# A convolution and two feed-forward layers in split float32: all low parts on the vector engine, and couples of 64-row products from unit 50 on

## The chip, the cores and the metric

The kernel runs on one core of a Trainium2 chip. The metric is the device time of one execution in microseconds, taken as the median of three runs. The engines that matter here are TensorE (PE, with its weight loads as PEld), the vector engine (DVE), the scalar engine (ACT), GpSimd (POOL) and the DMA queue of the sync engine (SP). Each engine works through its own instructions in the order in which they stand in the program, and waits on semaphores for what other engines must have done.

## The reference

```python
def reference(x, weight, moe_w_in, moe_w_out, moe2_w_in, moe2_w_out):
    # x: 2 x 4096 tokens x 192 channels; weight: 8 heads x 7 taps
    w = softmax(weight, axis=-1)                        # per head
    x = causal_conv(x, w)                               # 7 taps over time, per channel
    h = x @ moe_w_in                                    # 192 -> 2048
    g = where(h >= 1, h, where(h <= -1, 0, (h + 1) ** 2 / 4))
    x = g @ moe_w_out                                   # 2048 -> 192
    h = x @ moe2_w_in                                   # 192 -> 2048
    g = h / (1 + exp(-1.702 * h))
    return g @ moe2_w_out                               # 2048 -> 192
```

The four weight matrices are float64 arrays when they reach the chip. They are brought to float32 there, bit by bit, and every float32 operand of a product is then split into a high part (the value rounded to the type that TensorE multiplies in one pass) and a low part (the value less its high part). A product of two operands is the sum of high by high, high by low and low by high.

## The kernel before, in words

**Tiles, units and phases.** The 8192 tokens are cut into 16 blocks of 512 tokens. Activations lie with channels on partitions: 128 channels (the a part) and the other 64 (the b part). The hidden width of 2048 is cut into 16 slices of 128. A *unit* is one slice of one block in one layer: `gemm1` makes the hidden tile `h` (128 x 512, in one of four PSUM banks, chosen by the unit's number), `act_a` applies the nonlinearity and writes the tile `a`, `act_b` splits it into `ghi` and `glo`, and `gemm2` adds its product to the two banks of the block's output. A *phase* is one block in one layer, so 16 units. `phases` begins with (layer 1, block 0), (1, 1), (1, 2), (2, 0). The first 64 units take two phases in turn, four units of the one and four of the other: units 0 to 31 are phases 0 and 1, units 32 to 63 are phases 2 and 3. From unit 64 on phases follow one after the other.

**Two ways to multiply.** A whole unit (`gemm1`, `gemm2`) has 5 products each, on all 128 rows of TensorE. The other way (`gemm1_pieces`, `gemm2_pieces`, woven together by `both`) cuts each product in two halves of 64 rows. Two halves, one on the lower and one on the upper 64 rows, run at the same time as a couple. As the b part has only 64 channels, 38 halves (19 couples) do the work that two units need 20 whole products for. For this a block's b part must stand in both orders, high part on the lower rows (tile `xb`) and high part on the upper rows (tile `xc`). `swap_halves` makes the second tile from the first by two DMAs on SP's queue, and only for phases at or after the bound in `put_b` and `finish`. In `both`, the lower list begins with the pieces of the first unit and then those of the second; the upper list begins with those of `gemm2`.

**The order of the work is written out by hand.** Step `u` of the first loop issues `gemm1(u)`, `act_a(u)`, `act_b(u-1)`, `gemm2(u-4)`, perhaps `finish` of a phase, and then what `plan` holds for this step (`beside`). So DVE's order in a step is: the last operation of the activation of `u` (L274 in layer 1, L277 in layer 2), the low part `glo` of `u-1` (where DVE makes it), the three operations of `finish`, and the planned work. From `WHOLE` on a second loop takes two units a turn: `both(u, u-4)`, then `act_a` of `u` and `u+1`, `act_b` of `u` and `u+1`, `finish`, and then `beside(u)` and `beside(u+1)`.

**Planned work.** `weight_ops` turns one slice of a layer's weights (a weight tile) from float64 into its two parts in four pieces, one in each of four steps in a row: `begin` (ACT L118, DVE L119 and L120), `join` (DVE L126), `high_part` (ACT L131) and `low_part` (L135 and L136, on the engine `eng`). The tiles 4 to 7 of layer 1 begin one a step in the steps 2 to 5; from tile 8 of layer 1 on one tile begins every second step, in step 2f-9 for tile f of layer 1 and in step 27+2f for tile f of layer 2, the last in step 57. So tile 11 of layer 2 has its `low_part` in step 52 and is first used by unit 55, and tile 15 has it in step 60 and is first used by unit 63. `conv_at(1)` puts 14 taps of the convolution (L156, L157) and two splits into the steps 10 to 25. `finish` of phase 0 (layer 1, block 0) is in the steps 32 to 34; its last split writes the `xb` that unit 36 reads. `finish` of phase 1 is in the steps 36 to 38.

**Who makes low parts.** `split` has ACT copy the high part and then DVE subtract it, or another engine if it is given one. In `act_b` that is POOL for the units below `EARLY` (48). For weight tiles it is DVE for tile 0 and the tiles 4 to 7 of layer 1 and the odd tiles of layer 2, and POOL for all others.

Of the kernel before, what the change touches and what calls it, by code (L numbers as in the profile page):

```python
# [20 lines left out]
def kernel(  # L21
# [21 lines left out]
    nc = tc.nc  # L43
    NBLK, D, _ = out.shape
    K = taps_in.shape[2]
    NF, _, WC = w1.shape
    DB = D - P
    B = P // DB
# [1 line left out]
    H = P // 2  # L50
    LAG = 4
    CH = 4
    WHOLE = 4 * NF
    EARLY = 3 * NF

    const = ctx.enter_context(tc.tile_pool(name="const", bufs=1))
    wpool = ctx.enter_context(tc.tile_pool(name="wpool", bufs=1))
# [12 lines left out]
    def f32(ap):  # L70
        return ap.bitcast(F32)

    def split(src, hi, lo, eng=None):
        nc.scalar.copy(hi, src)  # L74
        (eng or nc.vector).tensor_sub(lo, src, f32(hi))  # L75


    taps = const.tile([P, 2, K], F32, name="taps")
# [20 lines left out]
        nc.sync.dma_start(s.rearrange("p c t -> p (c t)"), words[n][f].bitcast(U32))  # L99
        return s  # L100

    def weight_ops(n, f, s, eng):

        low, high = s[:, :, 0], s[:, :, 1]  # L110
        w = wt[n][:, f, :]
        m = WC - DB
        st = {}

        def begin():
            a = stage.tile([P, WC], F32, tag="wa", name="wa")
            d = stage.tile([P, WC], U32, tag="wd", name="wd", bufs=3)
            nc.scalar.mul(a, f32(high), 2.0**-112)  # L118
            nc.vector.tensor_single_scalar(d, low, 29, op=ALU.logical_shift_right)  # L119
            nc.vector.scalar_tensor_tensor(  # L120
                d, high, 0x80000000, d, op0=ALU.bitwise_and, op1=ALU.bitwise_or
            )
            st["a"], st["d"] = a, d

        def join():
            nc.vector.scalar_tensor_tensor(  # L126
                st["d"], st["a"].bitcast(U32), 3, st["d"], op0=ALU.logical_shift_left, op1=ALU.bitwise_or
            )

        def high_part():  # L130
            nc.scalar.copy(w[:, 0:WC], f32(st["d"]))  # L131

        def low_part():
            d = f32(st["d"])
            eng.tensor_sub(w[:, WC + DB : 2 * WC], d[:, 0:m], f32(w[:, 0:m]))  # L135
            eng.tensor_sub(w[:, WC : WC + DB], d[:, m:WC], f32(w[:, m:WC]))  # L136

        return [begin, join, high_part, low_part]

# [3 lines left out]
    def new_xs():  # L143
        return [xs_p.tile([P, T], F32R, tag=t, name=t) for t in ("xah", "xal", "xb", "xc")]
# [16 lines left out]
    def warm_up():  # L161

        w = bank(7, "warm")
        for _ in range(9):
            nc.tensor.matmul(w[:, 0:P], ident, ident, start=True, stop=True)
# [15 lines left out]
    def swap_halves(dst, src):  # L181
        nc.sync.dma_start(f32(dst[0:DB]), f32(src[DB:P]))
        nc.sync.dma_start(f32(dst[DB:P]), f32(src[0:DB]))

    def put_b(i, c):

        b, halved = i % B, phases.index((1, i)) * NF >= WHOLE
        t = x1[i][2 + (b if halved else 0)]
        hi, lo = (t[0:DB], t[DB:P]) if b == 0 else (t[DB:P], t[0:DB])
        split(c[b * DB : (b + 1) * DB], hi, lo)  # L190
        if halved:
            swap_halves(x1[i][3 - b], t)
# [22 lines left out]
    phases = [(1, 0), (1, 1), (1, 2), (2, 0)]  # L215
# [64 lines left out]
    def act_b(u):  # L280
        a = act.pop(u)
        hi = g_p.tile([P, T], F32R, tag="ghi", name="ghi")
        lo = g_p.tile([P, T], F32R, tag="glo", name="glo")
        split(a, hi, lo, nc.gpsimd if u < EARLY else nc.vector)
        halves[u] = (hi, lo)

    def acc_banks(p):
# [79 lines left out]
    def finish(p, step):  # L367
        n, i = phases[p]
        acc_a, acc_b = accs.pop(p)
        if n == 1:  # L370
            ah, al, b, c = x2[i] = new_xs()
            s = cv_p.tile([P, T], F32, tag="cva", name="s")
            nc.scalar.copy(s[0:DB], acc_b[DB:P])
            split(acc_a, ah, al)
            at(step + 1, lambda: nc.vector.tensor_add(s[0:DB], acc_b[0:DB], s[0:DB]))

            def put():
                split(s[0:DB], b[0:DB], b[DB:P])
                if phases.index((2, i)) * NF >= WHOLE:
                    swap_halves(c, b)  # L380

            at(step + 2, put)
        else:
            o = o_p.tile([P, 2, T], F32, tag="o", name="o")
            nc.scalar.copy(o[0:DB, 1], acc_b[DB:P])
            nc.scalar.copy(o[:, 0], acc_a)
            nc.vector.tensor_add(o[0:DB, 1], acc_b[0:DB], o[0:DB, 1])
            nc.sync.dma_start(out[i, 0:P], o[:, 0])
            nc.sync.dma_start(out[i, P:D], o[0:DB, 1])


    plan, xt, raw = {}, {}, {}

    def at(step, op):
        plan.setdefault(max(step, 0), []).append(op)

    def fetch_w(n, f):
        raw[n, f] = weight_load(n, f)

    def weights_at(n, f, eng):  # L400
        ops = []

        def piece():
            if (n, f) in raw:
                ops.extend(weight_ops(n, f, raw.pop((n, f)), eng))
            ops.pop(0)()

        return [piece] * 4

    def fetch_x(*which):  # L410
        for part, i in which:
            xt[part, i] = x_load(part, i)
# [11 lines left out]
    with tc.manual_schedule():  # L424
        nc.sync.dma_start(taps, taps_in)
        fetch_x((0, 0), (1, 0))
        fetch_w(1, 0)
        fetch_w(1, 1)
        fetch_x((0, 1))
        fetch_w(1, 2)  # L430

        make_identity(nc, ident)
        warm_up()
        softmax_taps()

        nc.scalar.activation(const.tile([P, 1], F32, name="table"), ident[:, 0:1], AF.Sigmoid)
        for i in range(B):
            x1[i] = new_xs()
        ca = cv_p.tile([P, T], F32, tag="cva", name="cva")
        cb_ps, ca_ps = bank(3, "cb_ps"), bank(2, "ca_ps")  # L440
        a0 = conv_taps(0, xt[0, 0], ca)
        b_ops = conv_on_pe(1, xt[1, 0], cb_ps, ident, nc.scalar.mul)
        a1 = conv_on_pe(0, xt[0, 1], ca_ps, ident, nc.gpsimd.tensor_scalar_mul)
        for op in b_ops:
            op()

        ws = [weight_ops(1, f, raw.pop((1, f)), nc.gpsimd if f else nc.vector) for f in range(CH - 1)]
        order = a0[0:3] + ws[0][0:1] + a0[3:5] + ws[0][1:3] + a0[5:7] + ws[0][3:4] + ws[1][0:1]
        order += [lambda: put_a(0, ca)] + ws[1][1:2] + [lambda: put_b(0, cb_ps)] + ws[1][2:] + ws[2]
        for op in order:  # L450
            op()
        fetch_w(1, 3)
        for k, op in enumerate(weights_at(1, 3, nc.gpsimd)):
            at(k // 2, op)
        for k, op in enumerate(a1):
            at((k + 2) // 3, op)
        at(1, lambda: put_b(1, cb_ps))
        at(2, lambda: put_a(1, ca_ps))

        def convert_at(n, f, steps):  # L460
            eng = nc.vector if (n, f) < (1, 2 * CH) or n == 2 and f % 2 else nc.gpsimd
            at(steps[0] - 3, lambda: fetch_w(n, f))
            for step, op in zip(steps, weights_at(n, f, eng)):
                at(step, op)

        for f in range(CH, NF):
            s = f - 2 if f < 2 * CH else 2 * f - 2 * CH - 1
            convert_at(1, f, range(s, s + 4))
        for f in range(NF):
            s = 2 * NF - 5 + 2 * f  # L470
            convert_at(2, f, range(s, s + 4))
        for j in range(1, NBLK // B):
            conv_at(j)

        def beside(step):
            for op in plan.get(step, []):
                op()

        def finish_if_last(u, step):
            if 0 <= u < len(units) and units[u][1] == NF - 1:  # L480
                finish(units[u][0], step)


        for step in range(WHOLE):
            gemm1(step)
            act_a(step)
            if step >= 1:
                act_b(step - 1)
            if step >= LAG:
                gemm2(step - LAG)  # L490
            finish_if_last(step - LAG - 1, step)
            beside(step)


        act_b(WHOLE - 1)
        for u in range(WHOLE, len(units) + LAG + 4, 2):
            v = u - LAG
            if u == WHOLE:
                finish_if_last(v - 1, u)
                gemm1(u)  # L500
                gemm2(v)
                gemm1(u + 1)
                gemm2(v + 1)
            elif u < len(units):
                both(u, v)
            elif v < len(units):
                gemm2(v)
                gemm2(v + 1)
            if u < len(units):
                for op in (act_a, act_b):  # L510
                    op(u)
                    op(u + 1)
            finish_if_last(v + 1, u + 1)
            for step in (u, u + 1):
                beside(step)
# [55 lines left out]
```

## Time and profile before

| what | value |
|---|---|
| median of 3 runs | 1163.39 us (1161.4 to 1163.95) |
| the profiled execution's own time | 1161.93 us |
| its span, first to last instruction | 1160.2 us |
| busy: PE, DVE, ACT, POOL | 1140.1, 898.7, 836.2, 108.9 us |
| granted TensorE clock, mean | 0.996 |

The page of the profile gives busy time of every engine over the span, a strip of 40 slices of 29 us, and groups of instructions. Busy time of PE is the time in which some product was in flight, and products overlap, so it does not show how many could have been started. The counts of products in a stretch do.

### The profile page before, as it was taken

What the parts mean: (1) busy time and instruction counts of PE and PEld (TensorE: products, weight loads), DVE (VectorE), ACT (ScalarE), POOL (GpSimd) and SP (SyncE); (2) the same over time, 40 slices, a digit from 0 to 9 for tenths busy, and PEclk for the clock granted to TensorE, in tenths of its full rate; (3) what the DMA queues carried; (4) which work ended last, traced back from release to release, by engine and by line L of the source; (5) the groups of instructions that cost most, each with busy time, mean ns of one, the idle gap of its engine ahead of it and who ended that gap; (6) DMA issues with size and microseconds to landing.
All of it is one profiled execution on the core that took longest, in us unless ns stands there. A gap on an engine that the chain in (4) does not pass through costs nothing.

```text
span 1160.2 us, 22918 instructions
## 1 busy us (share of the span) xinstructions
PE 1140.1 (98%) x9180; PEld 929.5 (80%) x9180; DVE 898.7 (77%) x1354; ACT 836.2 (72%) x1467; POOL 108.9 (9%) x99
## 2 busy tenths in 40 slices
PE   8988999999999999999999999999999999999998
PEld 5766788888888888888888888888888888888886
DVE  7998999678686886869768796777868688686765
ACT  6778787676867768676776867768686775867764
POOL 5677730000000000000000000000000000000000
PEclk9999999999999999999999999999999999999999
DMA  4321321010001000010000100001000100000000
GB/s 149 129 80 54 99 64 33 2 41 20 15 20 42 1 20 15 19 42 8 27 10 11 42 11 24 10 10 42 19 15 19 42 1 19 15 19 15 10 15 14
DMA packets 16378, 36.15 MB, mean 31 GB/s; under 512 B 2448, under 2 KB 2448, under 8 KB 16272
## 3 DMA queue, kind: packets, MB, share of 16 engines
q1 hardware_dynamic: 16272, 34.69, 10.1%
q8 instruction: 72, 1.18, 0.4%
q14 instruction: 34, 0.28, 0.1%
HBM read 21.05 MB, written 6.29 MB: 24 GB/s over the span
## 4 chain that ended last, share of the span: by engine, by line
PE 91%; DVE 3%; POOL 2%; ACT 2%; issue 1%; DMA 0%; SPq 0%; POOLq 0%; DVEq 0%; ACTq 0%
PE acc L359 44%; PE h L359 39%; PE h L250 4%; POOL glo L75 1%; PE acc L310 1%; PE acc L311 1%; PE acc L313 1%; PE acc L312 1%; PE acc L314 1%; DVE wd L126 1%; DVE wd L119 1%; POOL wt L135 0%; DVE a L274 0%; DVE wt L135 0%; DMA raw<-in_w_dram 0%
## 5 line engine op out<-in xcount | busy, mean ns | idle before, releaser
L359 PE MATMUL acc<-ghi,wt 64*128 64x512 f32 x2676 | 810.4, 386 | 0.0
L359 PE MATMUL h<-xah,wt 64*128 64x512 f32 x1784 | 688.9, 386 | 0.0
L359 PE MATMUL acc<-glo,wt 64*128 64x512 f32 x1784 | 658.7, 387 | 0.0
L359 PEld LDWEIGHTS acc<-ghi,wt 64*128 64x128 f32 x2676 | 455.9, 184 | 51.5
L74 ACT CAST ghi<-a 128x512 fp32r<-128x512 f32 x512 | 313.9, 616 | 109.6 <-DVE a L277 73.5
L359 PEld LDWEIGHTS acc<-glo,wt 64*128 64x128 f32 x1784 | 328.2, 184 | 37.8 <-DVE glo L75 2.8
L359 PEld LDWEIGHTS h<-xah,wt 64*128 64x128 f32 x1784 | 328.3, 184 | 35.3 <-issue 0.4
L359 PE MATMUL h<-xal,wt 64*128 64x512 f32 x892 | 344.4, 386 | 0.0
L75 DVE TENSOR_TENSOR glo<-a,ghi 128x512 fp32r<-128x512 f32 x464 | 313.1, 687 | 20.0
L274 DVE SCALAR_TENSOR_TENSOR a<-h,a 128x512 f32<-128x512 f32 x256 | 176.5, 689 | 154.4 <-ACT a L273 154.2
L359 PE MATMUL h<-xb,wt 64*128 64x512 f32 x669 | 223.9, 388 | 0.0
L359 PE MATMUL h<-xc,wt 64*128 64x512 f32 x669 | 222.8, 386 | 0.0
L277 DVE TENSOR_TENSOR a<-h,a 128x512 f32<-128x512 f32 x256 | 169.9, 686 | 55.1 <-ACT a L276 54.2
L276 ACT ACTIVATE a<-h 128x512 f32<-128x512 f32 x256 | 146.5, 594 | 82.9 <-PE h L359 77.3
L272 ACT ACTIVATE a<-h 128x512 f32<-128x512 f32 x256 | 151.0, 590 | 52.3 <-PE h L359 48.8
L359 PEld LDWEIGHTS h<-xal,wt 64*128 64x128 f32 x892 | 164.1, 184 | 17.4
L273 ACT ACTIVATE a<-a 128x512 f32<-128x512 f32 x256 | 161.8, 632 | 8.2
L359 PEld LDWEIGHTS h<-xc,wt 64*128 64x128 f32 x669 | 123.1, 184 | 16.6
L359 PEld LDWEIGHTS h<-xb,wt 64*128 64x128 f32 x669 | 122.3, 184 | 9.5
L75 POOL TENSOR_TENSOR glo<-a,ghi 128x512 fp32r<-128x512 f32 x48 | 67.2, 1405 | 40.1 <-ACT ghi L74 37.6
L157 DVE SCALAR_TENSOR_TENSOR cva<-xt,taps,cva 128x512 f32<-128x512 f32 x90 | 69.6, 773 | 1.3
L250 PE MATMUL h<-xah,wt 128*128 128x512 f32 x132 | 54.9, 416 | 8.5 <-POOL wt L135 5.6
(70 smaller groups left out, 719.5 us busy)
## 6 DMA issues: line engine op xcount, KB each, us to landing
raw<-in_w_dram SPq DMA_DIRECT2D x32, 448.0 KB, 3.3
xc<-xb SPq DMA_DIRECT2D x42, 128.0 KB, 2.2
xt<-in_xa_dram SPq DMA_DIRECT2D x16, 259.0 KB, 3.2
out_dram<-o SPq DMA_DIRECT2D x16, 256.0 KB, 2.0
xt<-in_xb_dram SPq DMA_DIRECT2D x8, 259.0 KB, 3.1
out_dram<-o SPq DMA_DIRECT2D x16, 128.0 KB, 2.3
xb<-xc SPq DMA_DIRECT2D x14, 128.0 KB, 2.2
taps<-in_taps_dram SPq DMA_DIRECT2D x1, 7.0 KB, 1.6
```

Of the source, the lines that this page charges most:

```text
L74: nc.scalar.copy(hi, src)
L75: (eng or nc.vector).tensor_sub(lo, src, f32(hi))
L119: nc.vector.tensor_single_scalar(d, low, 29, op=ALU.logical_shift_right)
L126: nc.vector.scalar_tensor_tensor(st["d"], st["a"].bitcast(U32), 3, st["d"], op0=ALU.logical_shift_left, op1=ALU.bitwise_or)
L157: return lambda: nc.vector.scalar_tensor_tensor(c, x, w, c, op0=ALU.mult, op1=ALU.add)
L250: nc.tensor.matmul(h, w, r, start=j == 0, stop=j == len(prods) - 1)
L272: nc.scalar.activation(a, h, AF.Relu, bias=0.5, scale=0.5)
L273: nc.scalar.activation(a, a, AF.Square)
L274: nc.vector.scalar_tensor_tensor(a, h, 1.0, a, op0=ALU.max, op1=ALU.min)
L276: nc.scalar.activation(a, h, AF.Sigmoid, scale=1.702)
L277: nc.vector.tensor_mul(a, h, a)
L359: mm = nc.tensor.matmul(banks[n], w, r, start=n in fresh, stop=ends.get(n) == k)
```

## The change

The bound from which units run as couples, `WHOLE`, goes from 64 to 48, so that the second loop begins with unit 48 (its first turn is still of whole products, and `both` is first called for the units 50 and 51, while two phases are still in turn). The bound from which a block's b part is kept in both orders becomes a constant of its own, `HALVED`, of 32 units, so block 2 in layer 1 and block 0 in layer 2 have it too. `EARLY` goes away, and with it every use of POOL for a low part: the 48 low parts `glo` of the first units and the low parts of 19 weight tiles are made by DVE.

```diff
-    WHOLE = 4 * NF
-    EARLY = 3 * NF
+    WHOLE = 3 * NF
+    HALVED = 2 * NF
...
-    def split(src, hi, lo, eng=None):
+    def split(src, hi, lo):
         nc.scalar.copy(hi, src)
-        (eng or nc.vector).tensor_sub(lo, src, f32(hi))
+        nc.vector.tensor_sub(lo, src, f32(hi))
...
-            eng.tensor_sub(w[:, WC + DB : 2 * WC], d[:, 0:m], f32(w[:, 0:m]))
-            eng.tensor_sub(w[:, WC : WC + DB], d[:, m:WC], f32(w[:, m:WC]))
+            nc.vector.tensor_sub(w[:, WC + DB : 2 * WC], d[:, 0:m], f32(w[:, 0:m]))
+            nc.vector.tensor_sub(w[:, WC : WC + DB], d[:, m:WC], f32(w[:, m:WC]))
...
-        b, halved = i % B, phases.index((1, i)) * NF >= WHOLE
+        b, halved = i % B, phases.index((1, i)) * NF >= HALVED
...
-        split(a, hi, lo, nc.gpsimd if u < EARLY else nc.vector)
+        split(a, hi, lo)
...
-                if phases.index((2, i)) * NF >= WHOLE:
+                if phases.index((2, i)) * NF >= HALVED:
                     swap_halves(c, b)
...
-        ws = [weight_ops(1, f, raw.pop((1, f)), nc.gpsimd if f else nc.vector) for f in range(CH - 1)]
+        ws = [weight_ops(1, f, raw.pop((1, f))) for f in range(CH - 1)]
...
-        for k, op in enumerate(weights_at(1, 3, nc.gpsimd)):
+        for k, op in enumerate(weights_at(1, 3)):
...
-            eng = nc.vector if (n, f) < (1, 2 * CH) or n == 2 and f % 2 else nc.gpsimd
             at(steps[0] - 3, lambda: fetch_w(n, f))
-            for step, op in zip(steps, weights_at(n, f, eng)):
+            for step, op in zip(steps, weights_at(n, f)):
                 at(step, op)
```

## Rows read from the trace of the kernel before

**Rows 1.** The page, part 2: busy tenths in 40 slices of 29 us.

```profile
PE   8988999999999999999999999999999999999998
...
DVE  7998999678686886869768796777868688686765
...
POOL 5677730000000000000000000000000000000000
```

**Rows 2.** Busy time by stretch: length, PE, PEld, DVE, ACT, POOL (xcount), PEclk, DMA.

```profile
19.10:44.90 25.80, 24.33 (x96) 17.45 (x95) 23.94 (x38) 21.65 (x40) 14.20 (x12) 1.00 0.44 142
44.90:93.40 48.50, 40.74 (x156) 29.63 (x156) 46.88 (x55) 37.23 (x68) 37.95 (x32) 0.95 0.20 67
93.40:118.40 25.00, 22.15 (x93) 17.90 (x92) 20.95 (x27) 21.90 (x40) 16.79 (x15) 0.96 0.24 75
...
130.00:160.00 30.00, 30.00 (x134) 24.86 (x133) 28.85 (x40) 23.56 (x44) 19.36 (x16) 1.00 0.37 116
...
300.00:800.00 500.00, 500.00 (x4408) 412.00 (x4406) 377.14 (x577) 364.34 (x634) 0.00 (x0) 1.00 0.08 21
```

**Rows 3.** Groups by line and form: POOL whole span, DVE 19 to 180 us.

```profile
L75 POOL TENSOR_TENSOR glo<-a,ghi 128x512 fp32r<-128x512 f32 x48 | 67.2, 1405 | 40.1 <-ACT ghi L74 37.6 <-PE h L250 2.5
L135 POOL TENSOR_TENSOR wt<-wd,wt 128x384 fp32r<-128x384 f32 x19 | 25.4, 1337 | 23.2 <-ACT wt L131 23.2
...
L274 DVE SCALAR_TENSOR_TENSOR a<-h,a 128x512 f32<-128x512 f32 x48 | 32.8, 683 | 7.6 <-ACT a L273 7.4
L126 DVE SCALAR_TENSOR_TENSOR wd<-wa,wd 128x448 uint32<-128x448 uint32 x29 | 29.7, 1024 | 0.1
L119 DVE TENSOR_SCALAR wd<-raw 128x448 uint32<-128x448 uint32 x29 | 24.8, 857 | 0.0
```

**Rows 4.** DVE in order of time: start us, us, line, operation; POOL idle here.

```profile
158.94 0.68 DVE L274 SCALAR_TENSOR_TENSOR a<-h,a 128x512 f32<-128x512 f32 x1
159.54 0.67 DVE L75 TENSOR_TENSOR glo<-a,ghi 128x512 fp32r<-128x512 f32 x1
160.14 0.38 DVE L119 TENSOR_SCALAR wd<-raw 128x448 uint32<-128x448 uint32 x1
160.55 0.63 DVE L120 SCALAR_TENSOR_TENSOR wd<-raw,wd 128x448 uint32<-128x448 uint32 x1
161.09 0.68 DVE L277 TENSOR_TENSOR a<-h,a 128x512 f32<-128x512 f32 x1
161.70 0.68 DVE L75 TENSOR_TENSOR glo<-a,ghi 128x512 fp32r<-128x512 f32 x1
162.29 0.55 DVE L135 TENSOR_TENSOR wt<-wd,wt 128x384 fp32r<-128x384 f32 x1
162.76 0.22 DVE L136 TENSOR_TENSOR wt<-wd,wt 128x64 fp32r<-128x64 f32 x1
162.90 0.62 DVE L126 SCALAR_TENSOR_TENSOR wd<-wa,wd 128x448 uint32<-128x448 uint32 x1
163.44 0.68 DVE L277 TENSOR_TENSOR a<-h,a 128x512 f32<-128x512 f32 x1
```

**Rows 5.** DVE and POOL in order of time, where both work.

```profile
143.32 1.72 DVE L126 SCALAR_TENSOR_TENSOR wd<-wa,wd 128x448 uint32<-128x448 uint32 x1
...
140.06 4.48 POOL L75 TENSOR_TENSOR glo<-a,ghi 128x512 fp32r<-128x512 f32 x3
```

**Rows 6.** DVE in order of time: a tap of the convolution, late.

```profile
197.46 0.75 DVE L157 SCALAR_TENSOR_TENSOR cva<-xt,taps,cva 128x512 f32<-128x512 f32 x1
```

**Rows 7.** PE in order of time: its waits at units 36 and 55.

```profile
118.15 0.73 PE L250 MATMUL h<-xb,wt 128*128 128x512 f32 x2 [2.85 <-DVE xb L75]
...
162.90 0.50 PE L250 MATMUL h<-xah,wt 128*128 128x512 f32 x1 [0.42 <-DVE wt L135]
```

**Rows 8.** ACT, then DVE, in order of time: unit 77, second of its couple turn.

```profile
214.28 0.60 ACT L276 ACTIVATE a<-h 128x512 f32<-128x512 f32 x1 [0.50 <-PE h L359]
...
215.52 1.47 DVE L75 TENSOR_TENSOR glo<-a,ghi 128x512 fp32r<-128x512 f32 x2
```

More of the change, by code (lines that the diff above doesn't have):

```diff
@@ L100, in weight_load, with weight_ops @@
         return s
-    def weight_ops(n, f, s, eng):
+    def weight_ops(n, f, s):
         low, high = s[:, :, 0], s[:, :, 1]
@@ L398, in fetch_w, with weights_at @@
         raw[n, f] = weight_load(n, f)
-    def weights_at(n, f, eng):
+    def weights_at(n, f):
         ops = []
@@ L404, in piece @@
             if (n, f) in raw:
-                ops.extend(weight_ops(n, f, raw.pop((n, f)), eng))
+                ops.extend(weight_ops(n, f, raw.pop((n, f))))
             ops.pop(0)()
```

## The prediction

> **What bounds the kernel now.** I began with the strip of busy tenths [rows 1]: from slice 7 on PE is busy throughout and POOL does nothing, so only the first six or seven slices (some 190 us) can lose time. There POOL is at work, and DVE stands at 8 or 9 tenths, higher than later. Next came busy time by stretch, for the counts [rows 2]. From 130 to 160 us PE runs whole products without a gap: 134 in 30 us, 0.226 us each (0.2266 by the spacing of starts), or 2.265 us for a unit's ten. From 44.9 to 93.4 us there are 156 where 48.5/0.2266 = 214 fit, and from 93.4 to 118.4 us 93 where 110 fit: 75 products or 17 us of PE are lost, while DVE is busy 46.88 of 48.5 us. So up to about 120 us DVE sets the pace. From there PE is busy without a gap but for one wait at unit 55, for a weight tile's low part [rows 7].
>
> Why DVE is late shows in the groups [rows 3]. Its weight conversions take 857 ns (L119) and 1024 ns (L126) on average until 180 us, yet with POOL idle the same lines take 0.38 and 0.62 [rows 4]. The pair of rows where both work tells why: L126 starts at 143.32 while POOL makes low parts from 140.06 to 144.54, and takes 1.72 us [rows 5]. It waited for POOL inside its own duration. L274, which reads one operand from PSUM, stays at 683 ns. The Trainium skill ("SBUF — State Buffer", Who interferes with whom) says that a vector instruction with two SBUF inputs and a GpSimd instruction that reads SBUF exclude each other for a whole instruction; L126 agrees, and by that rule all of the excess would go with POOL's work.
>
> **What moves to DVE, and what it gives back.** A DVE instruction that doesn't depend on the one before it starts about 0.08 us before that one's recorded end, so I price by spacing of starts [rows 4]: L274 or L277 0.60, `glo` 0.60, and a weight tile 0.41 + 0.54 + 0.47 + 0.14 + 0.54 = 2.10 us. Those rows are just what the changed kernel does in two steps: from 158.94 to 163.44, 4.50 us. PE needs 4.53 for two whole units, so DVE and PE are nearly level. Added to DVE: 48 `glo` x 0.60 = 28.8 and 19 tiles' low parts x 0.61 = 11.6, together 40.4 us. Given back: 29 x (1.024 - 0.62) = 11.7 on L126, 29 x (0.857 - 0.38) = 13.8 on L119, together 25.5, and something on the other lines that read SBUF alone. The two sums lie too near each other to settle the sign, so I sum DVE's work in stages up to one mark that both kernels have: the end of L135 of tile 11 of layer 2, in step 52, which unit 55 waits for. Before it ends at 162.84 [rows 4].
>
> Steps 0 to 8: 17 x 0.60, five tiles, three more weight pieces (1.5) and two splits (1.3) make 23.5; I take 23.8 for dependent neighbours. The stage takes 25.8 now [rows 2]. Steps 9 to 25: 34 x 0.60 = 20.4, seven tiles and a low part 15.3, fourteen taps 8.9 (0.75 less the overlap, 0.67 [rows 6]; the first of each chain has one operand, about 0.4), two splits 1.3: 45.9 against 48.5 [rows 2]. Steps 26 to 47: 44 x 0.60 = 26.4, tiles 0 to 8 and parts of 9 and 10 21.3, two `finish` of three 0.6 to 0.7 us operations 3.9: 51.6. Then `glo` of unit 47 (0.6), the turns of units 48 and 50 (2.5 + 2.1 and 3.1 + 2.1, since a layer-1 pair waits for ACT between its two L274), and turn 52 up to its L135 (2.6 + 0.55): 13.5. From 19.1 us this gives 19.1 + 23.8 + 45.9 + 51.6 + 13.5 = 153.9. **The mark comes 8.9 us earlier.** ACT has less to do (37.2 us busy of 48.5 [rows 2]). PE's wait at unit 36 [rows 7] is for DVE's step 34, and DVE still has step 35 to do meanwhile, so it costs DVE nothing.
>
> This holds if DVE never stands still. Each `glo` now stands right behind L274 or L277 in DVE's queue and waits for ACT's `ghi`; the weight pieces, the next L274 and so PE stand behind it. Lower bound: 0, as in rows 4, where nothing waits. Upper bound: the couples' pair of `glo` takes 1.47 us where 2 x 0.68 less 0.08 = 1.28 would do [rows 8], 0.19 a pair; if every one of 48 units lost as much as 0.16, 7.7 us. I take 1.0, near the lower bound, because rows 4 are the same sequence in the same stage.
>
> **The couples.** In the steady state 4408 half products in 500 us are 8.82 per us, 38 of them 4.31 us for two units [rows 2], against 4.53 for whole ones. Seven turns (units 50 to 63) become couples: 7 x 0.22 = 1.5 us at best. But the planned work keeps its step, and a turn now issues both units' activations and splits before it. Tile 11's low part, step 52, stands in DVE's queue behind `glo` of unit 53, which needs `h` of unit 53, complete only at the end of `both(52)`. `both(54)` follows at once and wants that low part for unit 55 after five couples, 1.1 us in. Rows 8 give the chain: unit 77's activation begins at 214.28 just after PE ends its `h`, and the second `glo` ends at 215.52 + 1.47 = 216.99, 2.7 us later; with 0.2 before it and L135's 0.55 behind it, 3.45 us. PE stands at least 3.45 - 1.1 = 2.3 us, and 3.2 by my sum of DVE, which comes to that turn with weight work of the last one. Tile 15 (step 60, used by unit 63 in `both(62)`) is the same. Before, in the first loop, unit 55 was three steps behind and still waited a little [rows 7], which shows how little slack the tile had.
>
> So behind the mark: before, eleven whole units (55 to 65) take 11 x 2.265 = 24.9 us up to the first couple. After, `both(54)` from its sixth couple 3.2, turns 56, 58, 60 12.9, five couples of `both(62)` 1.1, a stall of 2.3 to 3.2, the rest 3.2, turn 64 4.3: 27.0 to 27.9. **That gives back 2.1 to 3.0 us, say 2.4.** All behind this is the same code.
>
> The rest costs nothing: four more swap DMAs join SP's queue. The swap of block 2 waits for the split of step 25, and the fetch of tile 1 of layer 2, needed in step 29, stands behind it; four steps (9 us) cover that. Without the cover it would be the swap's few microseconds once. `xc` is wanted from unit 51 on. In startup the low parts of tiles 1 to 3 come from DVE a little sooner than POOL gave them; I count 0 to 0.7 us, taken at 0.
>
> **The sum.** 8.9 - 2.4 - 1.0 = 5.5 us. From the profiled execution's own 1161.9 us that is 1156.4; the median of the runs is 1.5 higher, 1163.4, and on it 1157.9. I put 1157.5.
>
> **The rivals.** *No stall at tiles 11 and 15.* If the low parts come in time, the 64-row turns give their 1.5 us, and PE alone counts behind unit 36, whose wait ends 9 us earlier (118.15 now [rows 7], about 109.2 by DVE's sum); with the wait at unit 55 and its slow products saved too, 9 to 12.5 us, 1151 to 1154.4. For: the wait is read from the program's order, no row shows it. Against: that order leaves no way round. Chance 0.15.
>
> *Lockstep.* DVE and ACT hand each unit to and fro and the `glo` waits lie nearer the 7.7 us: gain 3 down to -1, 1160.4 to 1164.4. Against: rows 4. Chance 0.2.
>
> *Slower: DVE's long durations are not POOL's doing* (or only partly). DVE is busy 97% of 44.9 to 93.4 [rows 2], and 40.4 us of work come to it; with durations as in rows 3, nearly all of it is added: up to 1204 us. Every microsecond of excess that stays costs one, so it decides from 5.5 us left, a fifth of what L126 and L119 alone would give back. Against: rows 4 and 5 show one line both ways, with POOL idle and busy. The Trainium skill ("Perfetto Trace Analysis", Optimizing Scalar/DVE Operations) says that with a saturated vector engine moving work to the scalar engine or even GpSimd may make sense; the change is the reverse of that, and by that advice alone the time would be this rival's. The same section warns that those two engines share a read port, so that moving work between them might not help, which the row of 1.72 us bears out. Chance 0.08, with some stalls of the kind at tile 11 on the tight tiles 10 and 14 in it.
>
> That the change does not do what it says is out: DVE's counts are in the code.
>
> **How the numbers follow.** Forecast (gain 3 to 8.5 us): 0.57; its own range is 1155 to 1160.4. With 0.15, 0.2 and 0.08 for the rivals, the range that leaves out 2 in 10 runs from 1152 (most of the first rival) to 1161.5 (part of lockstep). A difference of 0.2% (2.3 us) is about the least that can be told from no change. Faster by more: 0.57 + 0.15 + 0.08 from lockstep = 0.80; within: 0.12; slower: 0.08.
>
> **What would show it.** L119 at 0.38 and L126 at 0.62 all through, POOL without low parts; L135 of tile 11 near 154 us; PE idle in `both(54)` and `both(62)` for 2 to 3 us each with L135 as releaser; the couples of units 66 and 67 some 6 us earlier than now, when they begin at about 162.9 + 24.9 = 187.8. Wrong would be: DVE idle before most `glo`, or a wait of PE elsewhere of over 3 us after unit 36.

## The result, and the profile after

The changed kernel takes 1169.96 us (median; 1169.09 to 1172.91) where the kernel before takes 1162.43: a ratio of 1.0068, with a 95% interval of 1.0046 to 1.0091. It is slower by 7.5 us, or 0.7%. The forecast was 1157.5, in a range of 1152 to 1161.5. The profiled execution has a span of 1168.4 us against 1160.2, 8.2 us more.

The page, part 2, of the changed kernel (40 slices of 29 us; DVE and POOL as in [rows 1], and the granted clock of TensorE):

```profile
DVE  8999966779677786868768697777968688686665
...
POOL 2000000000000000000000000000000000000000
PEclk9999988999999999999999999999999999999999
```

POOL's work is gone, and DVE's row hardly rises for it: slices 1 to 5 hold 8 and 9 where they held 7 to 9, slices 6 and 7 have 6 where they had 9. But in the same slices 6 and 7 the granted clock of TensorE falls to 8, where it was 9 before.

Busy time by stretch, cut at the same events as [rows 2] (the first L274, those of units 9 and 26, PE's wait at unit 36, then the activation of unit 48, the end of turn 64, and the steady state):

```profile
19.10:42.95 23.85, 23.16 (x91) 16.59 (x90) 23.47 (x47) 21.52 (x40) 0.00 (x0) 1.00 0.45 149
42.95:89.07 46.12, 41.48 (x171) 32.48 (x170) 45.67 (x89) 37.09 (x68) 0.00 (x0) 0.96 0.16 52
...
111.30:142.00 30.70, 30.70 (x136) 25.40 (x137) 30.29 (x60) 23.82 (x45) 0.00 (x0) 1.00 0.39 122
142.00:196.40 54.40, 43.36 (x307) 34.80 (x307) 35.42 (x67) 30.50 (x55) 0.00 (x0) 0.81 0.08 26
...
300.00:800.00 500.00, 500.00 (x4408) 412.02 (x4406) 377.60 (x577) 364.89 (x635) 0.00 (x0) 1.00 0.08 21
```

The first two stages take 23.85 and 46.12 us where they took 25.8 and 48.5 [rows 2], PE's wait at unit 36 ends at 111.25 instead of 118.15 [rows 7], and then PE runs without a gap to 142. So far the change is a gain of 7 to 8 us. Everything is lost in the next row: from 142.0 to 196.4 us, the turns 48 to 64, PE is busy 43.4 of 54.4 us with 307 half products at a mean granted clock of 0.81. The steady state is the same as before.

DVE's groups from 19 to 180 us in the changed kernel (the lines of [rows 3]):

```profile
L274 DVE SCALAR_TENSOR_TENSOR a<-h,a 128x512 f32<-128x512 f32 x48 | 32.9, 685 | 7.5 <-ACT a L273 6.9
...
L126 DVE SCALAR_TENSOR_TENSOR wd<-wa,wd 128x448 uint32<-128x448 uint32 x28 | 17.3, 617 | 0.1
...
L119 DVE TENSOR_SCALAR wd<-raw 128x448 uint32<-128x448 uint32 x29 | 11.2, 385 | 0.0
```

L126 fell from 1024 to 617 ns and L119 from 857 to 385, while L274 stayed: with POOL silent the whole excess is gone. The Trainium skill ("SBUF — State Buffer", Who interferes with whom) has it so for L126, which reads two operands from SBUF; the rows agree. What L119, with one operand to read, had to wait for is not shown by these rows.

PE in order of time, its waits (the lines of [rows 7]; in brackets the idle time and what ended it):

```profile
111.25 0.73 PE L250 MATMUL h<-xb,wt 128*128 128x512 f32 x2 [3.51 <-DVE xb L75]
...
153.86 0.79 PE L359 MATMUL h<-xah,wt 64*128 64x512 f32 x1 [2.40 <-DVE wt L135]
159.32 0.79 PE L359 MATMUL h<-xah,wt 64*128 64x512 f32 x1 [2.89 <-DVE wt L135]
...
181.65 0.79 PE L359 MATMUL h<-xah,wt 64*128 64x512 f32 x1 [3.18 <-DVE wt L135]
...
186.58 0.79 PE L359 MATMUL h<-xah,wt 64*128 64x512 f32 x1 [2.37 <-DVE wt L135]
```

The waits for L135 that were forecast for tiles 11 and 15 are there (159.32 and 186.58), but the low parts of tiles 10 and 14 make PE wait too (153.86 and 181.65), and tile 14's 3.18 us is the longest wait of all. The waits from 140 to 200 us, with us in total, times and the longest, put five of PE's down to L135 (the fifth, for tile 13, is 0.21 us), and seven of ACT's to L126. PE has no other wait in this list:

```profile
ACT wt L131 <- DVE wd L126: 12.5, 7, 1.9
...
PE h L359 <- DVE wt L135: 11.0, 5, 3.2
```

One turn shows what makes them late. First DVE, then ACT, in order of time, in turns 50 and 52:

```profile
151.27 0.69 DVE L274 SCALAR_TENSOR_TENSOR a<-h,a 128x512 f32<-128x512 f32 x1 [0.46 <-ACT a L273]
151.88 1.46 DVE L75 TENSOR_TENSOR glo<-a,ghi 128x512 fp32r<-128x512 f32 x2
153.26 0.55 DVE L135 TENSOR_TENSOR wt<-wd,wt 128x384 fp32r<-128x384 f32 x1
...
153.86 0.62 DVE L126 SCALAR_TENSOR_TENSOR wd<-wa,wd 128x448 uint32<-128x448 uint32 x1
...
158.71 0.55 DVE L135 TENSOR_TENSOR wt<-wd,wt 128x384 fp32r<-128x384 f32 x1
...
148.85 0.57 ACT L272 ACTIVATE a<-h 128x512 f32<-128x512 f32 x1
...
150.61 0.63 ACT L273 ACTIVATE a<-a 128x512 f32<-128x512 f32 x1
...
152.00 0.62 ACT L74 CAST ghi<-a 128x512 fp32r<-128x512 f32 x1 [0.25 <-DVE a L274]
154.51 0.57 ACT L131 CAST wt<-wd 128x448 fp32r<-128x448 f32 x1 [1.90 <-DVE wd L126]
...
155.50 1.08 ACT L276 ACTIVATE a<-h 128x512 f32<-128x512 f32 x2
```

Read it as one chain. ACT's four operations for units 50 and 51 end at 151.24; DVE's second L274 follows, then both `glo`, then the low part of one tile (L135 and L136, the latter not shown) and the join of the next (L126), which ends at 154.48. ACT's high part (L131) is for that very join, so ACT stands 1.90 us, and behind L131 in its queue stands L118 (not shown), and behind that the activation of units 52 and 53. That begins at 155.50, 6.65 us after the one of turn 50. ACT and DVE take turns and neither can run ahead. Tiles begin in odd steps (27+2f), so a tile's join is in an even step and its high part in the odd step behind it; in the couples loop both steps are planned work of the same turn.

PE feels the chain only through the low parts. `both(52)` ends at 151.46, where the wait of 2.40 us begins, and tile 11's low part, behind the splits of turn 52, is done at 158.71 + 0.55 = 159.26, 7.8 us later.

### The profile page after: what moved, and what is told of

The parts are those of the page before. It is cut to its first block, busy times and chain, and to the rows that moved or that the text cites. A ratio compares the mean times of both kernels' runs of the same rounds, so it can differ in the third digit from the quotient of the medians.

```text
span 1168.4 us, 23144 instructions
## 1 busy us (share of the span) xinstructions
PE 1140.9 (98%) x9324; PEld 939.9 (80%) x9324; DVE 897.3 (77%) x1440; ACT 836.4 (72%) x1467; POOL 5.9 (1%) x13
## 4 chain that ended last, share of the span: by engine, by line
PE 87%; DVE 7%; ACT 4%; issue 1%; DMA 0%; SPq 0%; DVEq 0%; ACTq 0%
PE acc L359 44%; PE h L359 40%; DVE glo L75 2%; PE h L250 1%; DVE a L274 1%; DVE wd L126 1%; DVE wt L135 1%; ACT ghi L74 1%; ACT a L272 1%; ACT a L273 1%; DVE cva L157 1%; DVE wd L120 1%; ACT wa L118 0%; DVE wd L119 0%; DMA raw<-in_w_dram 0%
## 5 line engine op out<-in xcount | busy, mean ns | idle before, releaser
L359 PE MATMUL acc<-ghi,wt 64*128 64x512 f32 x2772 | 845.5, 388 | 0.0
L359 PE MATMUL h<-xah,wt 64*128 64x512 f32 x1848 | 717.8, 388 | 11.0 <-DVE wt L135 11.0
L359 PE MATMUL acc<-glo,wt 64*128 64x512 f32 x1848 | 686.4, 389 | 0.0
L359 PEld LDWEIGHTS acc<-ghi,wt 64*128 64x128 f32 x2772 | 476.3, 185 | 51.3
L359 PEld LDWEIGHTS h<-xah,wt 64*128 64x128 f32 x1848 | 342.2, 185 | 48.2 <-DVE wt L135 13.8
L359 PEld LDWEIGHTS acc<-glo,wt 64*128 64x128 f32 x1848 | 341.9, 185 | 37.5 <-DVE glo L75 2.8
L75 DVE TENSOR_TENSOR glo<-a,ghi 128x512 fp32r<-128x512 f32 x512 | 345.5, 687 | 20.8
L359 PE MATMUL h<-xal,wt 64*128 64x512 f32 x924 | 358.5, 388 | 0.0
L274 DVE SCALAR_TENSOR_TENSOR a<-h,a 128x512 f32<-128x512 f32 x256 | 176.6, 690 | 154.3 <-ACT a L273 153.7
L250 PE MATMUL h<-xah,wt 128*128 128x512 f32 x100 | 41.1, 411 | 4.4 <-DVE wt L135 4.4
L131 ACT CAST wt<-wd 128x448 fp32r<-128x448 f32 x32 | 18.1, 567 | 31.9 <-DVE wd L126 31.8
```

Of the source, the lines that this page charges most:

```text
L75: nc.vector.tensor_sub(lo, src, f32(hi))
L250: nc.tensor.matmul(h, w, r, start=j == 0, stop=j == len(prods) - 1)
L274: nc.vector.scalar_tensor_tensor(a, h, 1.0, a, op0=ALU.max, op1=ALU.min)
L359: mm = nc.tensor.matmul(banks[n], w, r, start=n in fresh, stop=ends.get(n) == k)
```

## The experiments

Three theories were set against each other. *Queue*: the chain above makes the turns long. *Due time*, the forecast's own: turns are long because PE waits for low parts that come one turn too late. *Load*: DVE has too much to do in a turn, now that all low parts are its own. The first two are not wholly apart, for by the chain the queue, too, reaches PE as late low parts.

The whole time of a run also holds what it gains or loses ahead of the couples. So a stretch is compared beside it: on PE, from the first couple of unit 50 to the first couple of unit 66, eight turns, in the one profiled execution of each kernel. It takes 53.9 us in the changed kernel.

### The low parts alone

```diff
-    WHOLE = 3 * NF
-    HALVED = 2 * NF
+    WHOLE = 4 * NF
+    HALVED = 4 * NF
```

> The low parts all on DVE, the couples as before from unit 66 on (both bounds at 64 units). All theories of the couples agree that the loss of the changed kernel lies in its couples turns 48 to 62. In the changed kernel unit 49 starts 8.5 us earlier on PE than before (140.17 against 148.72 us), and the wait of 0.8 us at unit 55 should go too: 1162.4 - 9.4 = 1153 us. If instead the low parts on DVE were themselves the cause of the loss, this run would lie above 1162.

Measured: 1153.89 us, 0.9935 of before (0.9919 to 0.9952). The row of DVE and PE behind unit 36 (busy time by stretch):

```profile
112.00:182.00 70.00, 69.52 (x301) 57.15 (x303) 66.14 (x129) 55.40 (x102) 0.00 (x0) 0.98 0.20 63
```

PE is busy 69.5 of 70 us while DVE makes every low part of that stretch: in the loop of whole products, where PE may be three units ahead of DVE, DVE keeps up. The first half of the change is a gain of 8.6 us. So DVE's load in that loop is not what lost the time.

### The couples alone

```diff
-    WHOLE = 4 * NF
+    WHOLE = 3 * NF
+    HALVED = 2 * NF
```

(with the two tests of `put_b` and `finish` against `HALVED`; POOL's low parts stay where they were before)

> The couples from unit 50 on and the b parts in both orders, but the low parts where they were (POOL below unit 48, and 19 weight tiles). Queue theory (ACT's high part of a weight tile waits in a turn for DVE's join, which stands behind both glo, and the next turn's activation stands behind it on ACT): the long turns of the changed kernel (6.1 to 8.1 us against 4.3) come back without the low parts, and the time is 1162.4 + 13 to 17 = 1175 to 1179 us. Due-time theory (only PE's wait for the low part of tiles 11 and 15): +4 to +6, 1167. Load theory (DVE has too much in a turn because the low parts were moved to it): turns near 4.5 us, about 1162.

Measured: 1176.80 us, 1.0131 of before (1.0114 to 1.0147). ACT in order of time in turns 48 and 50 (this kernel's lines are one further down):

```profile
156.09 0.56 ACT L132 CAST wt<-wd 128x448 fp32r<-128x448 f32 x1 [1.90 <-DVE wd L127]
...
157.08 0.59 ACT L273 ACTIVATE a<-h 128x512 f32<-128x512 f32 x1
```

The same 1.90 us wait of the high part, with the next activation behind it. The earlier couples cost 14.3 us by themselves, and the load theory, which gave 1162, falls. So does the due-time theory's 1167, which priced the stalls at their own length. The eight turns take PE 53.75 us here and 53.9 in the changed kernel: that DVE makes the low parts adds next to nothing to them. The two parts together make 14.3 - 8.6 = 5.7 of the 7.5 us.

### Weight tiles one step earlier

```diff
-            s = 2 * NF - 5 + 2 * f
+            s = 2 * NF - 6 + 2 * f
```

> The changed kernel with every weight tile of layer 2 one step earlier (26+2f in place of 27+2f). Begin and join of a tile then fall in one couples turn and high and low part in the next, so ACT waits for nothing on DVE that stands behind the glo of its own turn, and tile 11's low part is in turn 50, one turn ahead of its use. DVE's work in a turn is the same. Queue theory and due-time theory: turns of 4.3 to 4.7 us, 1151 to 1154 us. Load theory: turns stay over 6 us, about 1168.

Measured: 1154.34 us, 0.9934 of before (0.9919 to 0.9950). One step decides 15.6 us. ACT in order of time, the same turn as above:

```profile
152.55 0.62 ACT L74 CAST ghi<-a 128x512 fp32r<-128x512 f32 x1 [0.25 <-DVE a L274]
153.07 0.56 ACT L131 CAST wt<-wd 128x448 fp32r<-128x448 f32 x1
...
154.06 0.57 ACT L276 ACTIVATE a<-h 128x512 f32<-128x512 f32 x1
...
158.74 1.08 ACT L276 ACTIVATE a<-h 128x512 f32<-128x512 f32 x2
...
163.42 0.60 ACT L272 ACTIVATE a<-h 128x512 f32<-128x512 f32 x1
```

Turns 52 and 54 take 4.68 us each by their first activations (154.06, 158.74, 163.42). L131 starts right behind `ghi`, for its join was made in the turn before. ACT's wait for L126 between 140 and 200 us, 12.5 us in the changed kernel, is 1.1 here (waits, us in total, times, longest):

```profile
ACT wt L131 <- DVE wd L126: 1.1, 1, 1.1
```

But this step also brings tile 11's low part one turn ahead of its use, so by itself it doesn't tell queue from due time. It takes the load theory out once more, since DVE's work in a turn is unchanged.

### Weight tiles four steps earlier

```diff
-            s = 2 * NF - 5 + 2 * f
+            s = 2 * NF - 9 + 2 * f
```

> The changed kernel with every weight tile of layer 2 four steps earlier (23+2f): all low parts are now two turns and more ahead of their use, but join and high part of a tile are still in one turn, in the turns 48 to 56. Due-time theory: no wait of PE for a low part is left, 1152 us. Queue theory: those five turns stay at 6 us and more, the three behind them are at 4.3: 5 x 6.4 + 3 x 4.3 = 45 us against 53.4 in the changed kernel, about 1161 us.

Measured: 1161.02 us, 0.9991 of before (0.9982 to 1.0001). Here no low part is late, and ACT's wait is still there (waits from 140 to 200 us; the second is the whole of PE's list):

```profile
ACT wt L131 <- DVE wd L126: 9.8, 6, 1.9
...
PE acc L359 <- ACT ghi L74: 0.6, 2, 0.4
```

The time meets the queue theory's 1161, but by luck: its sum had 45 us from the activation of unit 48 to that of unit 64, and the trace has 39.4 (148.33 to 187.73). What fills the difference was lost ahead of the couples. PE in order of time at unit 36, first in this run and then with one step earlier:

```profile
116.58 1.22 PE L250 MATMUL h<-xb,wt 128*128 128x512 f32 x2 [6.20 <-DVE xb L75]
```

```profile
112.92 0.74 PE L250 MATMUL h<-xb,wt 128*128 128x512 f32 x2 [3.90 <-DVE xb L75]
```

Earlier weight tiles put more of DVE's work in front of the `xb` that unit 36 needs, and the first couple of unit 50 starts at 150.16 us here and at 145.83 with one step earlier, 4.3 us sooner. In the eight turns, without any wait for L135 and at a granted clock of 1.00, the queue by itself costs 3.3 us against one step earlier (38.22 and 34.95). So it is a cause of its own, but of 3 us and not of the 7 that the two medians lie apart.

### Weight tiles one step later

```diff
-            s = 2 * NF - 5 + 2 * f
+            s = 2 * NF - 4 + 2 * f
```

> The changed kernel with every weight tile of layer 2 one step later (28+2f). As with one step earlier, join and high part fall in different turns, so by the queue theory ACT isn't held up and turns without a wait for a low part take 4.7 us as in the run with one step earlier; but tile 11's low part (step 53) and tile 15's (step 61) are still in the turn just ahead of their use, and now behind the other tile's begin. So this run has the due-time stalls alone: two of 3 to 4 us, with products at half clock behind them, 1154.3 + 7 to 10 = 1161 to 1165 us. If the due times were harmless it would be at 1154.

Measured: 1165.61 us, 1.0029 of before (1.0016 to 1.0043). This run has the late low parts without the queue's chain. It lies 11.3 us over one step earlier, a little more than the 7 to 10 expected: PE waits for L135 four times from 140 to 200 us, not twice, 7.1 us in all:

```profile
PE h L359 <- DVE wt L135: 7.1, 4, 3.2
```

So late low parts are a cause of their own, and the larger one. The first loop doesn't explain it: tiles 3 and 7, one step nearer to their use, make PE wait 0.47 and 1.47 us there, but the wait at unit 36 is shorter (2.53 us), and the first couple of unit 50 starts at 144.31, ahead of one step earlier (145.83). The eight turns take 47.6 us, 12.7 more than with one step earlier. This is not the changed kernel's stall alone, for a low part stands here behind another tile's begin as well (L119 and L120, 0.41 + 0.54 = 0.95 us by the spacing of [rows 4]).

### The join ahead of the splits

```diff
-                for op in (act_a, act_b):
-                    op(u)
-                    op(u + 1)
+                act_a(u)
+                act_a(u + 1)
+                if u < 4 * NF:
+                    beside(u)
+                act_b(u)
+                act_b(u + 1)
             finish_if_last(v + 1, u + 1)
-            for step in (u, u + 1):
+            for step in (u, u + 1)[u < 4 * NF :]:
                 beside(step)
```

> The changed kernel with every weight piece in the step that it has there, but in the turns 48 to 62 the pieces of the first unit's step (low part of one tile, join of the next) are issued between the two activations and the two splits, not behind the splits. DVE's work in a turn and the turn in which each low part is made are unchanged. Queue theory: ACT's high part finds the join done, the next activation isn't held up, turns near 4.7 us, and what is left is PE's wait of about 1 us each for the low parts of tiles 11 and 15: 1155 to 1158 us. Load theory: turns stay over 6 us, 1168 to 1170.

Measured: 1157.67 us, 0.9953 of before (0.9935 to 0.9971). Every piece is in its turn and DVE's work is the same; only its place in the two queues differs, and 12.3 us of the changed kernel's time are gone. ACT's wait for the join, and PE's for the low part (140 to 200 us):

```profile
ACT wt L131 <- DVE wd L126: 4.1, 7, 1.1
...
PE h L359 <- DVE wt L135: 3.0, 2, 1.6
```

L131 waits 4.1 us in place of 12.5. PE still waits twice for a low part, 1.6 us at most, and the eight turns take 38.8 us in place of 53.9. But L135 stands ahead of both `glo` here as well as the join does, so this run eases the queue and the due times together and doesn't tell them apart.

### The four added swaps

```diff
-    WHOLE = 3 * NF
+    WHOLE = 4 * NF
```

> The changed kernel with the bound of the couples back at 64 units and the bound of the b parts in both orders left at 32: the low parts on DVE and the four added swap DMAs, without the earlier couples. The swaps were costed at nothing: 1153.9 us, as with the low parts alone. If they hold up a weight fetch or the 64-row turns lost their time to them, 1155 or more.

Measured: 1155.96 us, 0.9939 of before (0.9924 to 0.9955), beside 0.9935 (0.9919 to 0.9952) without the swaps. The median is 2.1 us higher, where the expectation put a cost of the swaps (1155 or more), but the intervals lie over each other. The two traces show no wait for a swap: PE waits 3.53 us at unit 36 with the swaps and 3.52 without, and both take 36.36 us from the first product of unit 50 to the first couple of unit 66. A cost of 2 or 3 us elsewhere is neither shown nor ruled out.

### Couples only once the weights are done

```diff
-    WHOLE = 3 * NF
+    WHOLE = 3 * NF + 8
...
-            s = 2 * NF - 5 + 2 * f
+            s = 2 * NF - 8 + 2 * f
```

> The changed kernel with every weight tile of layer 2 three steps earlier (24+2f, the last low part in step 57) and couples from unit 58 on, so that hardly a couples turn has weight work in it. Four turns (58 to 64) become couples at 4.31 us against 4.53: 0.9 us under the run with the low parts alone, 1153.0 us. If PE is held by DVE until unit 60 anyway, 1153.9.

Measured: 1157.47 us, 0.9954 of before (0.9941 to 0.9967), some 4 us over what was expected. PE in order of time at unit 36:

```profile
113.50 1.22 PE L250 MATMUL h<-xb,wt 128*128 128x512 f32 x2 [5.91 <-DVE xb L75]
```

Three steps earlier, the weight tiles put more of DVE's work in front of step 34, and PE's wait at unit 36 grows from 3.51 to 5.91 us, as it does with four steps earlier (6.20). What was planned for the end of the stage was lost in its middle. The kernels with the low parts alone and with one step earlier, 1153.9 and 1154.3, remain the fastest, and both beat the kernel before.

### The four places of the weight work side by side

The runs that only shift the weight tiles, and the changed kernel, cross the two causes. Busy time by stretch over the eight turns: the changed kernel, one step later, four steps earlier, one step earlier (one line of each run):

```profile
142.53:196.43 53.90, 42.86 (x306) 34.63 (x306) 34.95 (x66) 29.96 (x54) 0.00 (x0) 0.81 0.09 26
```

```profile
144.31:191.93 47.62, 40.53 (x306) 32.27 (x307) 33.93 (x65) 29.05 (x53) 0.00 (x0) 0.86 0.10 30
```

```profile
150.16:188.38 38.22, 37.33 (x304) 28.41 (x305) 29.03 (x54) 26.47 (x47) 0.00 (x0) 1.00 0.04 12
```

```profile
145.83:180.78 34.95, 34.93 (x307) 28.55 (x307) 32.06 (x61) 28.34 (x51) 0.00 (x0) 1.00 0.09 28
```

The eight turns in us, with the median of the whole kernel in brackets:

| tiles 11 and 15: low part | join and high part in one turn | in two turns |
|---|---|---|
| a turn ahead of its use, or more | 38.2 (1161.0, four steps earlier) | 35.0 (1154.3, one step earlier) |
| in the turn just ahead of its use | 53.9 (1170.0, the change) | 47.6 (1165.6, one step later) |

In the turns the queue alone costs 3.3 us over the best corner, late low parts alone 12.7, and both together 19.0, 3 us more than the sum of the two. That fits the chain, by which the queue makes low parts later still: PE's waits for them are 11.0 us with both causes and 7.1 with the due times alone. The cells are not cut quite clean. With four steps earlier ACT's wait of 1.90 us comes four times and not six, as the weight work ends sooner, and with one step later the low part also stands behind another tile's begin. So which cause is the larger is shown; their shares are rough.

## Why the prediction was wrong, point by point

**What bounds the kernel: right.** DVE set the pace up to unit 36 and its long durations were POOL's doing: L126 and L119 came out at the forecast 0.62 and 0.38. The rival that put them down to something else is dead.

**DVE's sum up to unit 48: right in kind, short by 1.4 us.** `glo` of unit 47 was summed to end the stage at 141.0, L274 of unit 48 starts at 143.40. Of these 2.4 us the 1.0 set aside for waits between ACT and DVE covers less than half. Up to unit 26 the sum is met within 0.3 us (L274 at 89.07, by the sum 88.8), so nearly all of it was lost in the steps 26 to 47 (the first stage's 23.85 us on a sum of 23.8 is in part luck, for five of the seven other kernels with the same code there take about 25); steps 29 and 31, for instance, measure 2.57 and 2.39 us for a sum of 2.15. The low parts alone gain 8.6 us, near the 8.9 less 1.0 of the sum.

**The couples: the step that failed.** In the sum, what lies behind the mark was to give back 2.4 us; it gave back 11.9. The forecast summed DVE's work by turn (4.6 us for turn 48, 5.2 for turn 50) and dismissed ACT with "ACT has less to do". ACT had less to do, but not the freedom to do it early. Spacing of the first activations is what a turn takes: turn 50 begins at 148.85 and turn 52 at 155.50. The later ones, ACT in order of time:

```profile
163.63 0.60 ACT L276 ACTIVATE a<-h 128x512 f32<-128x512 f32 x1 [2.57 <-PE h L359]
...
169.97 0.58 ACT L272 ACTIVATE a<-h 128x512 f32<-128x512 f32 x1
...
176.63 0.58 ACT L272 ACTIVATE a<-h 128x512 f32<-128x512 f32 x1
...
182.77 1.08 ACT L276 ACTIVATE a<-h 128x512 f32<-128x512 f32 x2
190.90 0.60 ACT L276 ACTIVATE a<-h 128x512 f32<-128x512 f32 x1 [5.56 <-PE h L359]
...
195.57 0.60 ACT L276 ACTIVATE a<-h 128x512 f32<-128x512 f32 x1
```

So the turns take 6.65, 8.13, 6.34, 6.66, 6.14, 8.13 and 4.67 us from turn 50 on, against the forecast 4.3, or 6.6 to 7.5 where a low part is late. The forecast read the order of DVE's queue, found the low parts of tiles 11 and 15 in it, and did not read ACT's queue the same way, in which L131 stands in front of the next turn's activation. And it counted a late low part at the length of PE's wait, for two tiles, where four tiles made PE wait and products at half the clock followed.

**The mark.** L135 of tile 11 in step 52 was forecast to end at 153.9, 8.9 us earlier than before. It ends at 159.26 (PE goes on at 159.32), 3.6 us earlier. Of the 5.4 us missing, 2.4 were there at unit 48 and the rest came in turns 48 and 50.

**Behind the mark.** Forecast 27.0 to 27.9 us up to the couples of unit 66, measured about 37.1 (159.3 to 196.43), before 25.2 (162.90 to 188.06). That is 11.9 us lost instead of 2.1 to 3.0, and with 3.6 gained before it gives 8.3, about the 8.2 us of the two spans.

The two stalls were right in place. That they are right in size too (2.89 and 2.37 us against 2.3 to 3.2) is luck. The forecast had 3.45 us from the end of `both(52)` to tile 11's low part, less 1.1 for five couples. Measured are 7.8 us, of which PE spends 2.40 waiting for tile 10 and 2.6 on five couples at half the clock (153.86 to 156.43), so that the rest looks like the forecast's stall.

The long turns of ACT and DVE (54, 56 and 58, 6.1 to 6.7 us) don't show on PE at once: its turns 56 and 58 take the forecast 4.3 us each (first couples at 164.82, 169.14 and 173.45). They show as tile 14's wait, which the sum put at nothing. From the end of `both(60)` at 178.47, where that wait begins, to PE going on at 186.58 with tile 15's low part there are 8.1 us, where the forecast had 3.4 to 4.3 for the five couples and the stall. Not forecast either was the clock: behind both waits TensorE is at the lower of its two levels, 1.2 GHz. The two rows (busy time by stretch) from the waits at 159.32 and 186.58 on:

```profile
159.30:164.05 4.75, 4.73 (x22) 3.75 (x24) 1.56 (x4) 1.51 (x3) 0.00 (x0) 0.50 0.00 0
186.56:191.36 4.80, 4.78 (x22) 3.78 (x24) 0.10 (x1) 0.46 (x1) 0.00 (x0) 0.50 0.00 0
```

22 halves, 11 couples, in 4.75 us at half the clock are 0.43 us a couple, where 0.2266 was counted: 11 x 0.2 = 2.2 us each, 4.5 in all on top of the stalls. The two together are 8 to 9 of the 9 to 10 us that are missing behind the mark.

**The rivals.** The sign came out on the side of the rival "slower", but by another mechanism. The nearest thing to the truth was its last clause, further waits at the tight tiles 10 and 14, which are at 153.86 and 181.65. Tile 14's 3.18 us is also the forecast's own sign of being wrong, a wait elsewhere of over 3 us. *Lockstep* had the right mechanism, ACT and DVE handing work to and fro, and the wrong place: it was put at every `glo` of the first loop, where it cost little, and not at L131 in the couples' turns. *No stall at tiles 11 and 15* is what one step earlier made true, and its 1154.3 us lies in that rival's 1151 to 1154.4.

## What to carry to other kernels

When an order by hand is regrouped, follow every engine's queue through one group and look for an instruction that waits for another engine's last work of the same group: what stands behind it starts after both engines are done, and their times add up where a sum by engine lets them overlap. Work planned by step number keeps its number when steps are taken in pairs, so which pieces share a pair is part of the change; here one step cost or saved 15.6 us, more than either half of the change. Don't price a wait of TensorE by its own length alone: look in the rows at which clock the products behind it run. And compare runs in the stretch that an edit is about: the run with four steps earlier met its forecast and had lost more than half of the time elsewhere. And if an engine's operations take longer beside another engine than alone, work moved to it may cost nothing: by estimate 40 us of low parts went to the engine that set the pace, and it finished sooner.

## What the runs showed of the hardware that was not expected

A couple of two 64-row products takes about as long as one whole product, 0.227 us (4408 halves in 500 us, against 0.2266 from start to start of whole products), so couples gain only what the halved b part saves, 19 couples for 20 products, 0.22 us a turn. Where nothing is late PE gets that gain: with one step earlier the stretch takes 34.95 us, and the same 16 units as whole products take 36.36 with the low parts alone, 1.4 us more (the forecast had 1.5 at best). ACT's and DVE's turns with weight work take 4.68 us there, longer than PE's 4.31, so in such turns they fall behind PE; over these eight it was busy 34.93 of the 34.95 us all the same. The medians of the two kernels, 1154.3 and 1153.9, are too near each other to show the gain.

TensorE's granted clock stood at 0.50 twice in the changed kernel, over 10 us each time (busy time by stretch):

```profile
153.80:164.05 10.25, 7.30 (x32) 5.52 (x34) 6.25 (x14) 4.79 (x9) 0.00 (x0) 0.50 0.15 46
181.12:191.36 10.24, 7.35 (x32) 5.55 (x34) 4.33 (x10) 3.23 (x6) 0.00 (x0) 0.50 0.00 0
```

As each began PE had been waiting for a low part (2.40 and 3.18 us), and within each it waited again (2.89 and 2.37); in each it ran only 32 halves. With one step earlier, where PE hardly waits, the same turns run at 1.00. So in these two places a stall of PE cost more than its own length.
